# The last two batches' product of decayed scores and v: plain float32 in place of bfloat16 pieces

## The chip, the cores and the metric

The kernel runs on one core of a Trainium2 chip. A core has TensorE (PE, matmuls; its weight loads are listed apart as PEld), VectorE (DVE), ScalarE (ACT), GpSimd (POOL) and SyncE (SP, which here only issues DMAs). Each engine works through its own instructions in the order in which the program gives them and waits on semaphores for the others; the DMA queue of SP also issues in order. The metric is device microseconds of the whole program, lower is better.

## The reference, cut to what matters

A gated linear attention (mLSTM) over 4 batches, 8 heads, 768 steps, head size 40, followed by an MLP mixer over tokens and channels:

```python
for t in range(S):                       # per batch and head
    m_new = np.maximum(f[t] + m, i[t])
    f_s, i_s = np.exp(f[t] + m - m_new), np.exp(i[t] - m_new);  m = m_new
    C = f_s * C + i_s * outer(v[t], k[t])
    n = f_s * n + i_s * k[t]
    y[t] = sigmoid(o[t]) * (C @ q[t]) / np.maximum(abs(n @ q[t]), 1.0)
# x = y as (batch, 768, 320)
u = x + (relu(x.T @ w_tok1) @ w_tok2).T
out = u + relu(u @ w_ch1) @ w_ch2
```

All of it is float32. The changed step is a part of `C @ q[t]` (and `n @ q[t]`, which is a column of ones appended to v).

## The kernel before, in words

The recurrence is done in chunks of 128 steps, 6 chunks to a batch, 24 units `(b, c)` in all. For one unit: `st_s` multiplies k with q (scores, tile `ps_sc`, 8 heads) and lets DVE multiply them with the decays (tile `dd`, 128 x 8 x 128, made by ACT's exponentials in `prep_exp` from rows that a DMA spreads over the partitions, after POOL has masked them in `prep_mask`). `st_state` multiplies the state `C` with the decayed q (`q3t`, line 316, batches 0 and 1 only) and forms the chunk's own update `pu` from the decayed k (`kw`) and v (line 324), which DVE folds into the next state `Cn`. `st_pv` multiplies the decayed scores with v, per head a 128x128 stationary tile and 41 columns (40 of v and the ones), and adds the state's part; ACT copies the result to `ht`, POOL multiplies it with the output gate (`st_hs`), DVE divides and rounds it (`st_x`), POOL forms the rounding's rest `xl` for the MLP's matmuls.

Batches 0 and 1 do `st_pv` in plain float32 (line 364). Batches 2 and 3 (`three(u)` true) split both sides into bfloat16 pieces whose sum is the float32 number: DVE makes the rests of the scores (`prep_p2`, line 281; `prep_p3`, line 289) and the three pieces of v (`prep_v`, lines 297 to 300), and `st_pv3` runs four bfloat16 matmuls per head (line 345; two of 82 columns, two of 41) into two PSUM tiles, adds the state's part there (line 350), and ACT and DVE add the halves (lines 352, 353).

The MLP of a batch is one stream on PE: `a_part` and `phase_b` (token mixing), transposes, then 18 slots of `gemm1` (tile `ps_h`) and `gemm2` (tile `acc`). ACT and DVE make `gh` and `gl` out of `ps_h` in between, for the `gemm2` of the slot after. The attention of the next batch is a generator, `att`, with 5 steps per unit; a table, `STEPS`, says how many of them follow each `gemm1`. So batch 2's attention runs inside batch 1's MLP, batch 3's inside batch 2's, and the order on every engine is fixed by where the steps call their operations:

- step 1: `st_s` and its products; step 2: `st_state`; step 3: first half of the next unit's exponentials; step 4: `st_pv`, `st_hs`; step 5: second half of the exponentials, loads for the unit after the next.
- for batches 0 and 1 the next unit's `prep_q3` and `prep_kw` (ACT's exponential of `pq`; POOL's `decay`, `q3t`, `kw`) stand in step 3 and `st_x` in step 4. For batches 2 and 3 they stand in step 5, behind `prep_v` and `st_x`.

Buffers: `dd` has two buffers and a third under the name `p12`, which batches 2 and 3 use for the rest `r`; `pq`, `kw` and `ht` have one, `q3t` and the k and v tile `kvt` two, the PSUM tag `m` (for `po`, `pu`, `ps_b`, some transposes) two.

Of the kernel before, what the change touches and what calls it, by code (L numbers as in the profile page):

```python
# [7 lines left out]
F32 = mybir.dt.float32  # L8
F32R = mybir.dt.float32r
I32 = mybir.dt.int32  # L10
BF16 = mybir.dt.bfloat16
# [6 lines left out]
L = 128  # L18
# [15 lines left out]
def kernel(ctx: ExitStack, tc: tile.TileContext, gates, qk, q3, kv, og,  # L34
# [148 lines left out]
    def load_phi(u):  # L183
        b, c = u
        T.setdefault(u, {})
        third = b < 2 and c % 3 == 2
        dd = ap.tile([128, H, L], F32, tag="p12" if third else "dd", name="dd", bufs=1 if third else 2)
        if b:
            nc.sync.dma_start(out=dd, in_=phi_d[c, b * HP:b * HP + H].partition_broadcast(128))
        T[u]["dd"] = dd  # L190
# [79 lines left out]
    def three(u):  # L270
        return u[0] > 1

    def prep_p2(u):
        t = T[u]
        dd = t["dd"]
        r = ap.tile([128, H, L], F32, tag="p12", name="r", bufs=1)
        p3 = xpool[1].tile([128, H, L], BF16, tag="p3", name="p3", bufs=1)
        t["p"] = (top(dd), top(r), p3)
        for hf in range(2):
            h = slice(4 * hf, 4 * hf + 4)  # L280
            nc.vector.tensor_tensor(r[:, h], dd[:, h], top(dd)[:, h], ALU.subtract)
        t["r"] = r

    def prep_p3(u):
        t = T[u]
        r, p3 = t["r"], t["p"][2]
        for hf in range(2):
            h = slice(4 * hf, 4 * hf + 4)
            nc.vector.tensor_tensor(p3[:, h], r[:, h], top(r)[:, h], ALU.subtract)

    def prep_v(u):
        t = T[u]
        vx = t["kv"][:, DM:]
        w = xpool[1].tile([128, 3, H * E1], BF16, tag="v3", name="v3", bufs=1)
        r = ap.tile([128, H * E1], F32, tag="kw", name="vr", bufs=1)
        v = nc.vector
        v.tensor_copy(w[:, 0], vx)
        v.tensor_tensor(r, vx, w[:, 0], ALU.subtract)
        v.tensor_copy(w[:, 1], r)
        v.tensor_tensor(w[:, 2], r, w[:, 1], ALU.subtract)  # L300
        t["v"] = w

# [3 lines left out]
    def st_state(u):  # L306
# [4 lines left out]
        if c > 0 and not three(u):  # L311
            pool = (ps_acc, "acc") if b == 0 and c % 2 else (ps_m, "m")
            po = pool[0].tile([128, H, E1], F32, tag=pool[1], name="po")
            pof = po.rearrange("p h e -> p (h e)")
            for g, (h0, n) in enumerate(GR):
                nc.tensor.matmul(pof[:, h0 * E1:(h0 + n) * E1], t["q3"][0][0:n * D, g, :],  # L316
                                 Cst[b][0:n * D, g * G3:g * G3 + n * E1], start=g == 0, stop=False)
            t["po"] = po
# [17 lines left out]
    def st_pv3(u):  # L336
        b, c = u
        t = T[u]
        p, w = t["p"], t["v"].rearrange("p j (h e) -> p h j e", h=H)
        ht = ap.tile([128, H, E1], F32, tag="ht", name="ht", bufs=1)  # L340
        for h0, h1 in ((0, 6), (6, 8)):
            po = ps_m.tile([128, h1 - h0, 2, E1], F32, tag="m", name="po")
            for h in range(h0, h1):
                for i, j0, j1 in ((0, 0, 2), (1, 0, 2), (0, 2, 3), (2, 0, 1)):
                    nc.tensor.matmul(po[:, h - h0, 0:j1 - j0], p[i][:, ROW[h], :], w[:, h, j0:j1],  # L345
                                     start=h == h0 and i + j0 == 0,
                                     stop=c == 0 and h == h1 - 1 and i == 2)
            for g, (g0, n) in enumerate(GR):
                if c and h0 <= g0 < h1:
                    nc.tensor.matmul(po[:, g0 - h0:g0 - h0 + n, 0], t["q3"][0][0:n * D, g, :],  # L350
                                     t["C"][0:n * D, g * G3:g * G3 + n * E1], start=False, stop=g > 0)
            nc.scalar.activation(ht[:, h0:h1], po[:, :, 0], AF.Copy)
            nc.vector.tensor_tensor(ht[:, h0:h1], po[:, :, 1], ht[:, h0:h1], ALU.add)  # L353
        t["ht"] = ht

    def st_pv(u, copy=True):
# [3 lines left out]
        if "p" in t:  # L360
            return st_pv3(u)
# [71 lines left out]
    def att(b):  # L433
        for c in range(NC):
            u = (b, c)
            n1, n2 = after(u, 1), after(u, 2)
            th = three(u)
# [5 lines left out]
            if n2 and not three(u):  # L443
                load_phi(n2)
            if n1 and not three(u):
                prep_mask(n1)
            if n2:
                load_qk(n2, 0)
            if th:
                prep_p2(u)  # L450
            yield
            if th:
                prep_p3(u)
            st_state(u)
            if n1 and three(u):
                prep_mask(n1)
            yield
            if n1:
                prep_exp(n1, 0)
                if not three(n1):  # L460
                    prep_q3(n1)
                    prep_kw(n1)
# [5 lines left out]
            if not th:  # L468
                st_x(u)
            yield  # L470
            if n1 and three(n1):
                prep_v(n1)
            if th:
                st_x(u)
            if n1:
                if three(n1):
                    prep_q3(n1)
                    prep_kw(n1)
                prep_exp(n1, 1)
            if n2:  # L480
                load_kv(n2)
                load_q3(n2)
                if three(u):
                    load_phi(n2)
# [534 lines left out]
```

## Time and profile before

| | |
|---|---|
| median of 3 runs | 468.4 us (465.58, 468.4, 473.29) |
| profiled execution, its own time | 468.86 us |
| span of the profile | 467.0 us, granted PE clock 0.977 on average |
| PE busy | 445.9 us (95%) |
| DVE, ACT, POOL busy | 314.1, 178.2, 137.8 us |

The profile's first 130 us hold batch 0's attention and the decoding of the weights, and 130 to 180 us batch 1's attention inside batch 0's MLP. Batch 2's attention runs from 184 to 280 us, batch 3's from 280 to 382 us. After that comes batch 3's MLP alone. A matmul's own duration says little about its cost: matmuls are pipelined and several are under way at a time. What one costs is read from the starts, from its own to that of the matmul behind it. A float32 matmul leaves two records, so eight of them are listed as x16.

### The profile page before, as it was taken

The page shows a single profiled execution, that of the slowest core. Times are in us where ns is not written, and L with a number is a line of the kernel's source. Part 1 is how long each engine was busy: PE and PEld are TensorE (multiplying, and loading weights), DVE is VectorE, ACT ScalarE, POOL GpSimd, SP SyncE. Part 2 cuts the span into 40 slices and gives each one's busy share as a digit, 9 for nine tenths or more (in the row PEclk, how much of TensorE's full clock was granted, in tenths as well). Part 3 has the DMA queues.
Part 4 walks back from the last instruction along what each step waited for, and adds up shares of the span by engine and source line. Part 5 has one row for each costly group of instructions (what it writes and reads, how often), then busy time and mean ns, then how long its engine had stood idle before and what let it go on. Part 6 is the DMA issues. An engine that isn't in the chain of part 4 may idle for free.

```text
span 467.0 us, 9350 instructions
## 1 busy us (share of the span) xinstructions
PE 445.9 (95%) x3674; PEld 426.3 (91%) x3674; DVE 314.1 (67%) x688; ACT 178.2 (38%) x440; POOL 137.8 (29%) x164
## 2 busy tenths in 40 slices
PE   7699899998999999999999999999999999999997
PEld 3698799897999999999988999999988999999996
DVE  5857999999267666877797578877689565223322
ACT  4544643764544545433224324514323411212111
POOL 5636763444315434022234123023133120000000
PEclk9999758999999999999999999999999999999999
DMA  7746765664038882222533822240542100000000
GB/s 228 218 128 219 211 170 201 225 197 145 2 133 213 223 262 96 86 57 80 163 82 98 257 66 76 71 113 23 162 124 63 39 1 29 1 0 29 1 28 29
DMA packets 25032, 53.16 MB, mean 114 GB/s; under 512 B 2577, under 2 KB 13781, under 8 KB 24989
## 3 DMA queue, kind: packets, MB, share of 16 engines
q1 hardware_dynamic: 24941, 52.46, 37.3%
q8 instruction: 29, 0.48, 0.4%
q14 instruction: 14, 0.11, 0.1%
q10 hardware_dynamic: 48, 0.11, 0.1%
HBM read 48.51 MB, written 4.04 MB: 113 GB/s over the span
## 4 chain that ended last, share of the span: by engine, by line
PE 64%; DMA 11%; DVE 8%; issue 6%; POOL 5%; ACT 4%; SPq 1%; POOLq 0%; DVEq 0%; ACTq 0%
PE ps_h L582 18%; PE acc L582 18%; DMA dd<-phi_d 7%; PE ps_a L582 5%; PE po L364 5%; PE ps_b L582 4%; PE ps_sc L258 4%; PE pu L324 2%; DMA pq<-phi_d 2%; DVE wf L555 2%; PE po L316 2%; PE po L345 2%; POOL q3t L226 1%; POOL dd L230 1%; ACT dd L238 1%
## 5 line engine op out<-in xcount | busy, mean ns | idle before, releaser
L582 PE MATMUL ps_h<-uT,c1h 128*128 128x256 f32 x720 | 138.2, 280 | 0.1
L582 PEld LDWEIGHTS ps_h<-uT,c1h 128*128 128x128 f32 x720 | 115.1, 189 | 1.1 <-DVE uT L633 0.3
L582 PE MATMUL ps_h<-uT,c1l 128*128 128x256 f32 x432 | 110.2, 279 | 0.0
L650 DVE SCALAR_TENSOR_TENSOR gl<-ps_h,gh 128x512 fp32r<-128x512 f32 x72 | 49.5, 687 | 81.0 <-ACT gh L649 80.9
L649 ACT ACTIVATE gh<-ps_h 128x512 fp32r<-128x512 f32 x72 | 42.9, 596 | 159.4 <-PE ps_h L582 150.4
L582 PE MATMUL acc<-c2h,gh 128*128 128x320 f32 x288 | 90.3, 321 | 0.0
L582 PE MATMUL acc<-c2l,gh 128*128 128x320 f32 x288 | 86.6, 308 | 0.0
L582 PEld LDWEIGHTS ps_h<-uT,c1l 128*128 128x128 f32 x432 | 81.3, 188 | 0.0
L582 PE MATMUL acc<-c2h,gl 128*128 128x320 f32 x288 | 65.9, 310 | 3.0 <-DVE gl L650 3.0
L238 ACT ACTIVATE dd<-dd,bcol 128x128 f32<-128x128 f32 x144 | 45.9, 392 | 31.0 <-POOL dd L230 30.9
L582 PEld LDWEIGHTS acc<-c2h,gh 128*128 128x128 f32 x288 | 54.1, 188 | 1.3
L582 PEld LDWEIGHTS acc<-c2l,gh 128*128 128x128 f32 x288 | 54.2, 188 | 0.0
L582 PEld LDWEIGHTS acc<-c2h,gl 128*128 128x128 f32 x288 | 47.9, 188 | 4.5 <-DVE gl L650 4.5
L384 POOL TENSOR_TENSOR sig<-sig,ht 128x320 f32<-128x320 f32 x23 | 19.6, 851 | 78.6 <-DVE ht L353 64.2
L416 POOL TENSOR_TENSOR xl<-x,xh 128x320 fp32r<-128x320 f32 x23 | 21.1, 919 | 49.5 <-DVE xh L412 43.6
L230 POOL TENSOR_SCALAR_AFFINE_SELECT dd<-dd 128x1024 f32<-128x1024 f32 x18 | 20.7, 1150 | 49.1 <-DMA dd<-phi_d 42.9
L268 DVE TENSOR_TENSOR dd<-ps_sc,dd 128x512 f32<-128x512 f32 x48 | 31.1, 681 | 4.8 <-PE ps_sc L258 4.8
L258 PE MATMUL ps_sc<-raw 40*128 40x128 f32 x384 | 33.2, 310 | 0.7 <-DMA raw<-in_qk_dram 0.7
L258 PEld LDWEIGHTS ps_sc<-raw 40*128 40x128 f32 x384 | 28.1, 210 | 5.0 <-DMA raw<-in_qk_dram 1.7
L364 PE MATMUL po<-kvt,dd 128*128 128x41 f32 x192 | 29.7, 324 | 1.2 <-issue 1.2
L364 PEld LDWEIGHTS po<-kvt,dd 128*128 128x128 f32 x192 | 29.2, 239 | 1.6 <-issue 1.3
L324 PE MATMUL pu<-kvt,kw 128*120 128x123 f32 (+1 forms) x120 | 18.3, 295 | 4.9 <-POOL kw L248 4.8
(127 smaller groups left out, 775.7 us busy)
## 6 DMA issues: line engine op xcount, KB each, us to landing
dd<-phi_d SPq DMA_DIRECT2D x18, 512.0 KB
wst<-in_wc_dram SPq DMA_DIRECT2D x22, 384.0 KB
kvt<-in_kv_dram SPq DMA_DIRECT2D x24, 324.0 KB
raw<-in_qk_dram SPq DMA_DIRECT2D x48, 160.0 KB
sig<-in_og_dram SPq DMA_DIRECT2D x8, 480.0 KB
out_dram<-x SPq DMA_DIRECT2D x24, 160.0 KB
q3t<-in_q_dram SPq DMA_DIRECT2D x20, 180.0 KB
pq<-phi_d SPq DMA_DIRECT2D x18, 180.0 KB
```

Of the source, the lines that this page charges most:

```text
L230: nc.gpsimd.affine_select(dd, dd, pattern=[[0, H], [1, L]], compare_op=ALU.is_ge, fill=-1e30, base=0, channel_multiplier=-1)
L238: nc.scalar.activation(dd[:, h, :], src[hf][:, h % 4, :] if src else dd[:, h, :], AF.Exp, bias=bcol[:, c, HP * b + h:HP * b + h + 1])
L258: nc.tensor.matmul(t["s"][hf][:, h, :], r[:, 1, h, :], r[:, 0, h, :], start=True, stop=True)
L268: nc.vector.tensor_tensor(dd, t["s"][hf], dd, ALU.mult)
L316: nc.tensor.matmul(pof[:, h0 * E1:(h0 + n) * E1], t["q3"][0][0:n * D, g, :], Cst[b][0:n * D, g * G3:g * G3 + n * E1], start=g == 0, stop=F ...
L324: nc.tensor.matmul(pu[0:n * D, g, 0:n * E1], kwf[:, h0 * D:(h0 + n) * D], vx[:, h0 * E1:(h0 + n) * E1], start=True, stop=True)
L364: nc.tensor.matmul(po[:, h, :], t["dd"][:, ROW[h], :], vx[:, h * E1:(h + 1) * E1], start=c == 0 and h == 0, stop=h == H - 1)
L384: (nc.vector if u == (0, NC - 1) else nc.gpsimd).tensor_tensor(sg, sg, ht[:, :, 0:D], ALU.mult)
L416: (nc.vector if u == (0, 4) else nc.gpsimd).tensor_tensor(xl, x, f32(xh), ALU.subtract)
L582: nc.tensor.matmul(ps, a, m, start=(first and i == 0), stop=(last and i == n - 1))
L649: nc.scalar.activation(gh, ps, AF.Relu)
L650: nc.vector.scalar_tensor_tensor(gl, ps, 0.0, f32(gh), op0=ALU.max, op1=ALU.subtract)
```

## The change

`three`, `prep_p2`, `prep_p3`, `prep_v` and `st_pv3` are gone. All batches use `st_state` and `st_pv` as batches 0 and 1 did, and all units have the order of steps that batch 1 had: `prep_mask` and the load of `dd` in step 1, `prep_q3` and `prep_kw` in step 3, `st_x` in step 4. `dd` has three buffers of one tag throughout.

```diff
--- before.py
+++ after.py
@@ -183,8 +183,7 @@
     def load_phi(u):
         b, c = u
         T.setdefault(u, {})
-        third = b < 2 and c % 3 == 2
-        dd = ap.tile([128, H, L], F32, tag="p12" if third else "dd", name="dd", bufs=1 if third else 2)
+        dd = ap.tile([128, H, L], F32, tag="dd", name="dd", bufs=3)
         if b:
             nc.sync.dma_start(out=dd, in_=phi_d[c, b * HP:b * HP + H].partition_broadcast(128))
         T[u]["dd"] = dd
@@ -267,39 +266,6 @@
             dd = t["dd"][:, 4 * hf:4 * hf + 4, :]
             nc.vector.tensor_tensor(dd, t["s"][hf], dd, ALU.mult)
 
-    def three(u):
-        return u[0] > 1
-
-    def prep_p2(u):
-        t = T[u]
-        dd = t["dd"]
-        r = ap.tile([128, H, L], F32, tag="p12", name="r", bufs=1)
-        p3 = xpool[1].tile([128, H, L], BF16, tag="p3", name="p3", bufs=1)
-        t["p"] = (top(dd), top(r), p3)
-        for hf in range(2):
-            h = slice(4 * hf, 4 * hf + 4)
-            nc.vector.tensor_tensor(r[:, h], dd[:, h], top(dd)[:, h], ALU.subtract)
-        t["r"] = r
-
-    def prep_p3(u):
-        t = T[u]
-        r, p3 = t["r"], t["p"][2]
-        for hf in range(2):
-            h = slice(4 * hf, 4 * hf + 4)
-            nc.vector.tensor_tensor(p3[:, h], r[:, h], top(r)[:, h], ALU.subtract)
-
-    def prep_v(u):
-        t = T[u]
-        vx = t["kv"][:, DM:]
-        w = xpool[1].tile([128, 3, H * E1], BF16, tag="v3", name="v3", bufs=1)
-        r = ap.tile([128, H * E1], F32, tag="kw", name="vr", bufs=1)
-        v = nc.vector
-        v.tensor_copy(w[:, 0], vx)
-        v.tensor_tensor(r, vx, w[:, 0], ALU.subtract)
-        v.tensor_copy(w[:, 1], r)
-        v.tensor_tensor(w[:, 2], r, w[:, 1], ALU.subtract)
-        t["v"] = w
-
     Cst = {}
     GR = ((0, 3), (3, 3), (6, 2))
 
@@ -308,7 +274,7 @@
         t = T[u]
         vx = t["kv"][:, DM:]
         t["C"] = Cst.get(b)
-        if c > 0 and not three(u):
+        if c > 0:
             pool = (ps_acc, "acc") if b == 0 and c % 2 else (ps_m, "m")
             po = pool[0].tile([128, H, E1], F32, tag=pool[1], name="po")
             pof = po.rearrange("p h e -> p (h e)")
@@ -333,32 +299,10 @@
                                                    op0=ALU.mult, op1=ALU.add)
             Cst[b] = cn
 
-    def st_pv3(u):
-        b, c = u
-        t = T[u]
-        p, w = t["p"], t["v"].rearrange("p j (h e) -> p h j e", h=H)
-        ht = ap.tile([128, H, E1], F32, tag="ht", name="ht", bufs=1)
-        for h0, h1 in ((0, 6), (6, 8)):
-            po = ps_m.tile([128, h1 - h0, 2, E1], F32, tag="m", name="po")
-            for h in range(h0, h1):
-                for i, j0, j1 in ((0, 0, 2), (1, 0, 2), (0, 2, 3), (2, 0, 1)):
-                    nc.tensor.matmul(po[:, h - h0, 0:j1 - j0], p[i][:, ROW[h], :], w[:, h, j0:j1],
-                                     start=h == h0 and i + j0 == 0,
-                                     stop=c == 0 and h == h1 - 1 and i == 2)
-            for g, (g0, n) in enumerate(GR):
-                if c and h0 <= g0 < h1:
-                    nc.tensor.matmul(po[:, g0 - h0:g0 - h0 + n, 0], t["q3"][0][0:n * D, g, :],
-                                     t["C"][0:n * D, g * G3:g * G3 + n * E1], start=False, stop=g > 0)
-            nc.scalar.activation(ht[:, h0:h1], po[:, :, 0], AF.Copy)
-            nc.vector.tensor_tensor(ht[:, h0:h1], po[:, :, 1], ht[:, h0:h1], ALU.add)
-        t["ht"] = ht
-
     def st_pv(u, copy=True):
         b, c = u
         t = T[u]
         vx = t["kv"][:, DM:]
-        if "p" in t:
-            return st_pv3(u)
         po = t["po"] if c else ps_m.tile([128, H, E1], F32, tag="m", name="po")
         for h in range(H):
             nc.tensor.matmul(po[:, h, :], t["dd"][:, ROW[h], :], vx[:, h * E1:(h + 1) * E1],
@@ -434,54 +378,36 @@
         for c in range(NC):
             u = (b, c)
             n1, n2 = after(u, 1), after(u, 2)
-            th = three(u)
             if b + 1 < B and c in (3, 4):
                 load_sig(b + 1, c - 3)
             if b > 1 and c == 0:
                 sigmoid(b)
             st_s(u)
-            if n2 and not three(u):
+            if n2:
                 load_phi(n2)
-            if n1 and not three(u):
+            if n1:
                 prep_mask(n1)
             if n2:
                 load_qk(n2, 0)
-            if th:
-                prep_p2(u)
             yield
-            if th:
-                prep_p3(u)
             st_state(u)
-            if n1 and three(u):
-                prep_mask(n1)
             yield
             if n1:
                 prep_exp(n1, 0)
-                if not three(n1):
-                    prep_q3(n1)
-                    prep_kw(n1)
+                prep_q3(n1)
+                prep_kw(n1)
             if n2:
                 load_qk(n2, 1)
             yield
             st_pv(u)
             st_hs(u)
-            if not th:
-                st_x(u)
+            st_x(u)
             yield
-            if n1 and three(n1):
-                prep_v(n1)
-            if th:
-                st_x(u)
             if n1:
-                if three(n1):
-                    prep_q3(n1)
-                    prep_kw(n1)
                 prep_exp(n1, 1)
             if n2:
                 load_kv(n2)
                 load_q3(n2)
-                if three(u):
-                    load_phi(n2)
             yield
 
     def prep_first(u, n):
```

Two places where the order moves. The first is GpSimd, in batch 2, between the mask of one unit (`dd`) and the next; `sig` is `st_hs`, `xl` belongs to `st_x`, and `decay`, `q3t` and `kw` are made for the next unit. Before:

```order
L230 AFFINE_SELECT dd<-dd 128x1024
L384 TENSOR_TENSOR sig<-sig,ht 128x320
L416 TENSOR_TENSOR xl<-x,xh 128x320
L225 COPY decay<-pq 120x3
L226 TENSOR_TENSOR q3t<-q3t,pq 120x384
L248 TENSOR_TENSOR kw<-kvt,wcol 128x320
```

The change:

```order
L229 AFFINE_SELECT dd<-dd 128x1024
L224 COPY decay<-pq 120x3
L225 TENSOR_TENSOR q3t<-q3t,pq 120x384
L247 TENSOR_TENSOR kw<-kvt,wcol 128x320
L328 TENSOR_TENSOR sig<-sig,ht 128x320
L360 TENSOR_TENSOR xl<-x,xh 128x320
```

The next unit's `decay`, `q3t` and `kw` now come ahead of this unit's `sig` and `xl`, which need the result of `st_pv` and DVE's division.

The second place is TensorE in batch 2, unit (2, 1), steps 1 and 2. Before:

```order
L258 MATMUL ps_sc<-raw 128x128 x8
L324 MATMUL pu<-kvt,kw 120x123 x2
L324 MATMUL pu<-kvt,kw 80x82
L582 MATMUL acc_2458<-c2h,gh 128x320
L582 MATMUL acc_2458<-c2l,gh 128x320
```

The change:

```order
L257 MATMUL ps_sc<-raw 128x128 x8
L282 MATMUL po<-Cn,q3t 128x123 x2
L282 MATMUL po<-Cn,q3t 128x82
L290 MATMUL pu<-kvt,kw 120x123 x2
L290 MATMUL pu<-kvt,kw 80x82
L508 MATMUL acc_2412<-c2h,gh 128x320
```

The state's part (`po`) moves from among the bfloat16 matmuls of `st_pv3` to ahead of `pu`. At `st_pv` itself eight rows of float32 matmuls (128x41) stand where 32 bfloat16 ones were.

## Rows read from the trace of the kernel before

**Rows 1.** Windows: us, busy time (count) per engine, granted PE clock, DMA share, GB/s

```profile
130.00:180.00 50.00, 48.65 (x431) 46.34 (x430) 32.76 (x82) 22.83 (x66) 19.11 (x24) 1.00 0.71 205
180.00:284.00 104.00, 101.75 (x962) 98.52 (x961) 78.22 (x179) 39.49 (x98) 26.98 (x32) 1.00 0.37 112
284.00:384.00 100.00, 97.50 (x923) 95.23 (x922) 74.44 (x170) 32.91 (x86) 25.85 (x31) 1.00 0.25 72
```

**Rows 2.** Waits, 180 to 385 us: us in total, times, longest

```profile
PE pu L324 <- POOL kw L248: 4.8, 6, 1.1
...
PEld pu L324 <- POOL kw L248: 6.0, 6, 1.4
PEld ps_b L582 <- DVE rl L600: 0.4, 2, 0.2
```

**Rows 3.** Timeline of PE, unit (2, 2): start, duration, instruction, count

```profile
228.56 0.21 PE L345 MATMUL po<-v,dd 128*128 128x82 bf16 x1
...
229.33 0.69 PE L350 MATMUL po<-Cn,q3t 120*128 120x123 f32 x4
...
230.11 0.43 PE L350 MATMUL po<-Cn,q3t 80*128 80x82 f32 x2
230.34 0.39 PE L582 MATMUL acc<-c2h,gh 128*128 128x320 f32 x1
```

**Rows 4.** Timeline of PE, unit (2, 0), 32 bfloat16 matmuls between these

```profile
197.68 0.21 PE L345 MATMUL po<-v,dd 128*128 128x82 bf16 x1
...
198.71 0.39 PE L582 MATMUL acc<-c2h,gh 128*128 128x320 f32 x1
```

**Rows 5.** Timeline of PE, batch 1, units (1, 1) and (1, 3)

```profile
143.20 1.87 PE L364 MATMUL po<-kvt,dd 128*128 128x41 f32 x16
144.90 0.39 PE L582 MATMUL acc<-c2h,gh 128*128 128x320 f32 x1
...
157.80 0.79 PE L316 MATMUL po<-Cn,q3t 120*128 120x123 f32 x6
158.43 0.77 PE L324 MATMUL pu<-kvt,kw 128*120 128x123 f32 x6
159.03 1.92 PE L364 MATMUL po<-kvt,dd 128*128 128x41 f32 x16
```

**Rows 6.** Timeline of PE, one of the six waits for kw

```profile
358.39 0.83 PE L324 MATMUL pu<-kvt,kw 128*120 128x123 f32 x6 [0.90 <-POOL kw L248]
```

**Rows 7.** Timeline of POOL, the same stretch

```profile
355.23 0.88 POOL L416 TENSOR_TENSOR xl<-x,xh 128x320 fp32r<-128x320 f32 x1 [2.80 <-DVE xh L412]
...
356.19 1.02 POOL L226 TENSOR_TENSOR q3t<-q3t,pq 120x384 f32<-120x384 f32 x1
357.17 1.17 POOL L248 TENSOR_TENSOR kw<-kvt,wcol 128x320 f32<-128x320 f32 x1
```

**Rows 8.** Groups of DVE by shape: count, busy us, mean ns, idle before

```profile
L281 DVE TENSOR_TENSOR r<-dd 128x512 f32<-128x512 f32 x24 | 21.4, 929 | 0.0
...
L298 DVE TENSOR_TENSOR vr<-kvt,v 128x328 f32<-128x328 f32 x12 | 10.5, 874 | 1.5 <-DVE v L297 0.5
```

**Rows 9.** Timelines of SP, ACT and PE, unit (1, 5)

```profile
163.17 0.74 SPq L214 DMA_DIRECT2D pq<-phi_d  x1
...
171.77 0.53 ACT L222 ACTIVATE pq<-pq 120x384 f32<-120x384 f32 x1 [2.96 <-DMA pq<-phi_d]
...
175.69 2.08 PE L364 MATMUL po<-kvt,dd 128*128 128x41 f32 x16 [1.21 <-issue]
177.60 0.39 PE L582 MATMUL acc<-c2h,gh 128*128 128x320 f32 x1
```

**Rows 10.** Groups of PE by shape, whole span

```profile
L364 PE MATMUL po<-kvt,dd 128*128 128x41 f32 x192 | 29.7, 324 | 1.2 <-issue 1.2
...
L345 PE MATMUL po<-v,dd 128*128 128x82 bf16 x96 | 13.9, 200 | 0.0
...
L345 PE MATMUL po<-v,p 128*128 128x41 bf16 x96 | 13.3, 181 | 0.0
```

## The prediction

> **What bounds the kernel now.** I read the windows first, then the waits of TensorE in the stretch that the change touches, then TensorE's timeline there, and the other engines last. The windows [rows 1] are to show whether TensorE has anything to give away where batches 2 and 3 do their attention, 180 to 384 us. It has not: it is busy 101.75 of 104 and 97.50 of 100 us, at the full granted clock (1.00), while DVE is busy 75%, ACT 35% and POOL 26% of that time. Idle are 204 - 199.25 = 4.75 us, and the waits [rows 2] say what for: six waits for POOL's `kw`, 4.8 us together on the matmuls and 6.0 us on the weight loads ahead of them, nothing else on the matmuls' side. DVE, from which the change takes the most, does not appear there, but for 0.4 us before `ps_b`. So this stretch is issued by TensorE almost without a break, and the change has to be priced in what TensorE issues, plus those waits.
>
> **TensorE: what the product costs.** Durations of single matmuls mislead here; they overlap. The four bfloat16 groups of the 12 units add up to about 54 us of busy time (two like each of the two shown, 13.9 and 13.3), the float32 group of the other 12 units to 29.7 [rows 10]; read as costs, these would say that float32 is the cheaper by half. Starts tell otherwise.
>
> - Unit with c = 0 (2 of the 12): 32 bfloat16 matmuls go from 197.68 to 198.71, 1.03 us [rows 4]. Eight float32 ones, 16 records, go from 143.20 to 144.90, 1.70 us [rows 5]. That is +0.67 us, twice: +1.3.
> - Unit with c > 0 (10 of the 12): bfloat16 matmuls and the state's part together take 228.56 to 230.34, 1.78 us [rows 3]. After the change the state's part runs in one piece ahead of `pu`, as it does from 157.80 to 158.43, 0.63 us [rows 5], and the unit pays 0.63 + 1.70 = 2.33 us. That is +0.55 us, ten times: +5.5.
>
> Together TensorE issues 6.8 us more. The price of the float32 group is bounded by other places of the same line: 1.70 us is the lowest, 177.60 - 175.69 = 1.91 us behind a stall is the highest [rows 9], which would be 12 x 0.21 = 2.5 us more. I take 1.70, since in batches 2 and 3 the group follows a `gemm1` as it does at 143.20, and with no stall ahead of it.
>
> **TensorE: which waits go.** `kw` is late before because POOL takes it last of a row of five: `xl` first waits 2.80 us for DVE's rounding, and `q3t` and `kw` follow it, so that `kw` ends at 358.34 and `pu` starts at 358.39, 0.90 us late [rows 6, 7]. DVE's rounding in turn stands behind the splitting of v. After the change `q3t` and `kw` come in step 3, ahead of `st_pv` and of everything that needs its result, and `pu` uses `kw` in step 2 of the next unit. That is at least one slot of the MLP later, mostly two, so all six waits should go: -4.8 us by the one row, -6.0 by the other, and I take the middle, -5.4. The 0.4 us before `ps_b` [rows 2] are the MLP's `rl` behind the rests of scores on DVE; those are gone too: -0.4.
>
> **DVE, ACT, POOL: nothing on the path.** DVE loses its largest groups there, 21.4 and 10.5 us among them [rows 8], and the smaller ones of the split; ACT loses one of two copies per unit; POOL has as many operations as before in another order. No wait of TensorE's names DVE's split, but for those counted, so I cost this at nothing: what covered it is TensorE's own stream.
>
> **What is moved and waits anew.** `prep_q3` goes from step 5 to step 3. Its first operation, ACT's exponential of `pq`, waits for a DMA, and behind it on ACT are now the copy `ht` of this unit, the second half of the next unit's exponentials and the next `gh`; behind POOL's `q3t` are `kw` and `st_hs`, and DVE's `x` waits for that. With `pq` in time this costs nothing: the next `gl` is wanted by `gemm2` a whole slot later. `st_x` in step 4 makes DVE wait for ACT and POOL right behind `st_pv`, in front of the next `gl`; the same slot covers it. The load of `dd` in step 1 finds a free buffer of three, where two had to wait for `st_pv`; SP passes it ahead of the scores' operands instead of behind `pq`, and POOL's mask, one unit later, has that unit's time. The PSUM tile `po` is now held from step 2 to step 4; between these steps the table puts no other user of that tag but `pu`, which takes the second buffer. For batches 0 and 1 the third buffer is only renamed.
>
> **The sum.** 6.8 - 5.4 - 0.4 = +1.0 us on the profiled execution's 468.86 us (span 467.0): **469.9 us**, 1.5 us over the median of the runs shown. By the bounds above: 469.3 to 473.0.
>
> **A rule against the row.** The group of eight float32 matmuls has 192 records for 96 matmuls [rows 10], so two of 106 ns each per head [rows 5]. The Trainium skill (FP8 and Floating Point Precision, section TensorE Precision Notes) says that true float32 takes four passes through the array. With a weight load for each pass at the row's 106 ns the unit would pay 3.4 us, and the sum would be 12 x 1.7 = 20 us higher, 490 us. The trace shows two records, not four, and I go by it; 1% for more than two.
>
> **Rivals.**
>
> 1. **The wait for POOL stays.** POOL's three operations for the next unit now wait for ACT and `pq`, and `pu` and the state's matmuls wait for both `q3t` and `kw`. If step 3's POOL work still ends behind step 2 of the next unit, the 5.4 us stay: 475.3 us. Against it: POOL is busy a quarter of the time [rows 1], and has a slot more. 13%.
> 2. **`pq` comes late (slower).** In unit (1, 5) this order shows its weak side: `pq` issued at 163.17, ACT waits 2.96 us for it and begins at 171.77, 8.6 us after the issue, and the exponentials and the product behind it leave TensorE idle for 1.21 us ahead of `st_pv` [rows 9]. If each of the ten units with c > 0 does so, 12.1 us: 482.0 us. It decides where landing takes longer than the way from step 5 to step 3 of the next unit. For it: the order is the same. Against it: batch 1's units follow each other after (159.03 - 143.20) / 2 = 7.9 us [rows 5], batch 2's after (228.56 - 197.68) / 2 = 15.4 us [rows 3, 4], and the DMA share is 0.37 and 0.25 there, 0.71 in batch 1 [rows 1]. 6%.
> 3. **DVE's relief gives more than the waits show.** The weight loads idle 204 - 193.75 = 10.25 us; without the 6.4 us named, 3.8 us are left in short gaps. If they all came from a crowded DVE, 466.1 us. Against it: no row names it. 11%.
> 4. **Columns set the price (faster).** If a matmul cost what it streams, 4 x 41 = 164 columns a head against 246, the group would take 1.03 x 164 / 246 = 0.69 us, 12 x 1.01 us less than I count: 457.8 us. The two records at 106 ns each speak flatly against it [rows 5]. 2%.
>
> **Range and chances.** My case has 67%, at 469.9 us. 464.5 to 476 us takes in its bounds, rivals 1 and 3, and what the runs of one kernel differ by (the three shown lie 2.8 us under and 4.9 us over their median); rivals 2 and 4 stay out. Two per cent, about what a measurement can tell from no change, are 9.4 us: under 459.0 us only rival 4 and an unforeseen gain, 3%; over 477.8 us rival 2 and the four passes, 7%; within, 90%.
>
> **What would show it.** In the profile of the changed kernel: line 308 from its first start to the next line's, 1.70 us in batches 2 and 3 as in batch 1; line 282 ahead of `pu` at 0.63 us; no wait of `pu` for `kw` after 180 us; TensorE busy all but some 1 us there, and the stretch up to the last attention about 1 us longer; DVE's busy time lower by more than the 31.9 us of [rows 8], with no effect on the span. The prediction is wrong if TensorE idles ahead of `po` or `st_pv`, if ACT waits for `pq` by several us in batches 2 and 3, or if the float32 groups there start at another pace.

## The result, and the profile after

The changed kernel takes 471.04 us, the median of 20 runs (469.2 to 477.06), the kernel before 469.52 us in 20 runs beside it. The ratio is 1.0059, with a 95% interval of 1.0031 to 1.0087: 2.8 us more by the ratio, the same by the bound of 2%. (It is taken without the runs that lie over 1.5% above the fastest of their kernel, and is not the ratio of the two medians, 1.0032.) The forecast was 469.9 us in a range of 464.5 to 476 us, on a net cost of 1.0 us.

The profiled execution took 469.2 us (span 467.4), against 468.86. That difference of 0.3 us is not the change's alone: ahead of 180 us the runs differ by some microseconds, whichever kernel it is. I therefore compare the stretch that the change touches, from the first score matmul of unit (2, 0) to the first `ps_a` of batch 3's MLP: 183.94 to 383.97 us before, 181.66 to 384.39 us after, so 200.03 and 202.73 us, **2.70 us more**. What follows it to the end takes 83.07 and 82.99 us.

The page's first part, for the kernel after:

```profile
PE 447.1 (96%) x3482; PEld 429.7 (92%) x3482; DVE 264.0 (56%) x568; ACT 177.0 (38%) x428; POOL 135.5 (29%) x164
```

DVE has lost 314.1 - 264.0 = 50.1 us of work, and the kernel is no faster. The windows of [rows 1], after (the second and third cover nearly all of the stretch):

```profile
130.00:180.00 50.00, 49.57 (x438) 47.65 (x439) 33.15 (x79) 25.09 (x68) 21.25 (x27) 1.00 0.73 214
180.00:284.00 104.00, 103.03 (x858) 101.11 (x857) 52.05 (x116) 37.55 (x90) 25.85 (x33) 1.00 0.34 107
284.00:384.00 100.00, 99.03 (x816) 97.58 (x816) 48.47 (x109) 31.37 (x79) 21.61 (x28) 1.00 0.23 72
```

TensorE idles 204 - 202.06 = 1.94 us there, where it idled 4.75 us. It waits less and takes longer: it has more to issue. All that it waits for between 180 and 385 us, to be held against [rows 2]:

```profile
PEld pu L290 <- issue: 2.2, 2, 1.1
PE pu L290 <- DVE uT L560: 1.9, 2, 1.0
...
PEld ps_sc L257 <- issue: 0.6, 3, 0.2
```

No wait for `kw` is left, and none for `rl`. In their place stands something new: `pu`, twice, behind DVE's `uT`, which is a tile of the MLP. TensorE's timeline shows the product: the group of unit (2, 0), which answers to [rows 4], and steps 2 and 4 of unit (2, 2), which answer to [rows 3]:

```profile
194.94 1.87 PE L308 MATMUL po<-kvt,dd 128*128 128x41 f32 x16
196.64 0.39 PE L508 MATMUL acc<-c2h,gh 128*128 128x320 f32 x1
...
221.97 0.79 PE L282 MATMUL po<-Cn,q3t 120*128 120x123 f32 x6
...
226.90 1.88 PE L308 MATMUL po<-kvt,dd 128*128 128x41 f32 x16
228.60 0.39 PE L508 MATMUL acc<-c2h,gh 128*128 128x320 f32 x1
```

From start to start the float32 group takes 1.70 us in both, 16 records of 106 ns. Summed over the stretch, each instruction from its own start to the next one's, TensorE's time by tile is:

| tile | before, us | after, us | difference |
|---|---|---|---|
| `po` (product and state's part) | 19.90 | 29.44 | +9.54 |
| `ps_h` | 71.45 | 67.72 | -3.73 |
| `ps_t` | 5.92 | 3.76 | -2.16 |
| `pu` | 6.04 | 5.60 | -0.44 |
| `ps_b` | 11.38 | 10.91 | -0.47 |
| `acc`, `ps_sc`, `ps_a` | 85.33 | 85.29 | -0.04 |

The waits for `kw` lay behind whatever stood ahead of `pu`, `ps_h` or `ps_t`, so that their end shows there: -6.33 us with `pu` itself. 5.7 us of that are the six gaps ahead of `pu`, 0.75 to 1.40 us from start to start before and 0.11 or 0.12 us where nothing is waited for. Of the +9.54 us, 2.27 are the new wait and 7.27 the product with the state's part. In unit 3 of batch 2 the new wait stands between lines 282 and 290; TensorE first, then DVE:

```profile
237.75 0.27 PE L557 MATMUL ps_t<-id_t,xd 128*128 128x128 f32 x1
237.86 0.80 PE L282 MATMUL po<-Cn,q3t 120*128 120x123 f32 x6
239.62 0.80 PE L290 MATMUL pu<-kvt,kw 128*120 128x123 f32 x6 [0.97 <-DVE uT L560]
240.22 0.39 PE L508 MATMUL acc<-c2h,gh 128*128 128x320 f32 x1
```

```profile
238.04 0.69 DVE L576 SCALAR_TENSOR_TENSOR gl<-ps_h,gh 128x512 fp32r<-128x512 f32 x1 [3.05 <-ACT gh L575]
238.64 0.41 DVE L559 TENSOR_TENSOR uT<-ps_t,uT 128x256 fp32r<-128x256 f32 x1
239.07 0.29 DVE L560 TENSOR_TENSOR uT<-ps_t,uT 64x128 fp32r<-64x128 f32 x1
239.40 0.42 DVE L559 TENSOR_TENSOR uT<-ps_t,uT 128x256 fp32r<-128x256 f32 x1
```

At slot 9, which falls into unit 3 of either batch, the MLP transposes its block 4 into a buffer of PSUM tag `m`, just ahead of step 2. `po` takes the tag's other buffer, and `pu` has to wait for the first until DVE has read it: line 290 starts 1.76 us behind line 282 and not 0.63. Before the change `po` was opened only in step 4, and `pu` found the second buffer free: where its `kw` is early (e1_early_kw, below), it starts 0.11 us behind the transposes in the same unit.

### The profile page after: what moved, and what is told of

Its sections match the earlier page's. It is cut to its first block, busy times and chain, and to the rows that moved or that the text cites. A ratio compares the mean times of both kernels' runs of the same rounds, so it can differ in the third digit from the quotient of the medians.

```text
span 467.4 us, 8794 instructions
## 1 busy us (share of the span) xinstructions
PE 447.1 (96%) x3482; PEld 429.7 (92%) x3482; DVE 264.0 (56%) x568; ACT 177.0 (38%) x428; POOL 135.5 (29%) x164
## 4 chain that ended last, share of the span: by engine, by line
PE 83%; DMA 5%; DVE 5%; ACT 3%; issue 2%; POOL 1%; SPq 1%; ACTq 0%; DVEq 0%; POOLq 0%
PE ps_h L508 25%; PE acc L508 25%; PE po L308 10%; PE ps_sc L257 6%; PE ps_b L508 4%; PE ps_a L508 4%; PE po L282 3%; PE pu L290 3%; DVE wf L481 2%; DMA wst<-in_wt_dram 2%; DMA kvt<-in_kv_dram 2%; DMA raw<-in_qk_dram 1%; ACT wf L465 1%; DVE wf L485 1%; DMA wst<-in_wc_dram 1%
## 5 line engine op out<-in xcount | busy, mean ns | idle before, releaser
L308 PE MATMUL po<-kvt,dd 128*128 128x41 f32 x384 | 50.6, 296 | 0.3 <-ACT gh L575 0.3
L308 PEld LDWEIGHTS po<-kvt,dd 128*128 128x128 f32 x384 | 50.1, 210 | 0.7 <-ACT gh L575 0.4
L224 POOL COPY decay<-pq 120x3 f32<-120x3 f32 x16 | 4.4, 274 | 117.6 <-ACT pq L221 117.6
L360 POOL TENSOR_TENSOR xl<-x,xh 128x320 fp32r<-128x320 f32 x23 | 21.3, 925 | 24.7 <-DVE xh L356 21.5
L225 POOL TENSOR_TENSOR q3t<-q3t,pq 120x384 f32<-120x384 f32 x15 | 15.5, 1037 | 21.2 <-ACT pq L221 21.2
```

The lines of the kernel that those rows point to most:

```text
L225: (nc.vector if u[0] == 1 else nc.gpsimd).tensor_tensor(q3t, q3t, pq, ALU.mult)
L308: nc.tensor.matmul(po[:, h, :], t["dd"][:, ROW[h], :], vx[:, h * E1:(h + 1) * E1], start=c == 0 and h == 0, stop=h == H - 1)
L360: (nc.vector if u == (0, 4) else nc.gpsimd).tensor_tensor(xl, x, f32(xh), ALU.subtract)
```

## The experiments

All ratios are to the kernel before on the same chip. "Stretch" is the one defined above (before 200.03, after 202.73 us), each from one profile.

| run | ratio | 95% interval | stretch, us |
|---|---|---|---|
| e1_early_kw | 0.9922 | 0.9888 to 0.9956 | 195.37 |
| e2_old_order | 1.0071 | 1.0036 to 1.0107 | 203.12 |
| e3_other_bank | 1.0033 | 1.0002 to 1.0065 | 200.41 |
| e4_split_kept | 1.0179 | 1.0134 to 1.0225 | 205.67 |
| e5_f32_twice | 1.0615 | 1.0544 to 1.0685 | 227.27 |
| e6_bf16_twice | 1.0165 | 1.0114 to 1.0217 | 206.06 |
| e7_two_dd | 1.0072 | 1.0037 to 1.0108 | 202.68 |
| e8_early_kw_calm | 0.9899 | 0.9862 to 0.9936 | 195.37 |
| e9_other_bank_calm | 0.9994 | 0.9959 to 1.0029 | 200.47 |
| e10_early_kw_shift | 0.9935 | 0.9905 to 0.9965 | 196.17 |
| e11_shift32 | 1.0078 | 1.0045 to 1.0111 | 203.97 |
| e12_split_kept_clean | 1.0105 | 1.0053 to 1.0158 | 203.02 |

### The two halves apart: the order alone, the product alone

e1_early_kw is the kernel before with its bfloat16 pieces, and only `prep_q3` and `prep_kw` moved to step 3 (`vr` gets a buffer of its own, since it used that of `kw`):

```diff
                 prep_exp(n1, 0)
-                if not three(n1):
-                    prep_q3(n1)
-                    prep_kw(n1)
+                prep_q3(n1)
+                prep_kw(n1)
...
-                if three(n1):
-                    prep_q3(n1)
-                    prep_kw(n1)
                 prep_exp(n1, 1)
```

> Edit alone of the order: the kernel before, bfloat16 pieces and all, with prep_q3 and prep_kw of batches 2 and 3 in step 3 instead of step 5 (the rest of v, vr, gets a buffer of its own, since kw now lives across prep_v). My theory, that the changed kernel pays 6.8 us for the float32 product and gets most of it back from POOL's late kw: the six waits of pu go, 5.4 us less than the kernel before, ratio 0.988, and no wait comes in their place. Rival, that the waits go only when DVE loses the split: POOL's q3t and kw stay as late as they were or pass the wait on, ratio 1.000.

The stretch is 4.66 us shorter than before, and the run takes 0.8% less, between the theory's 0.988 and the rival's 1.000. TensorE's waits in it:

```profile
PEld L345 <- DVE p L289: 0.5, 2, 0.3
PEld ps_b L578 <- DVE rl L596: 0.4, 2, 0.2
...
PE po L345 <- DVE p L289: 0.3, 2, 0.2
```

The waits for `kw` are gone and 0.3 us for the pieces have come. So the order alone removes them, and nothing of float32 is needed for it. It does not show in full: by tiles, `po` takes 0.65 us more than before, and `gemm1` some 1.1 us more for another reason ("where the operands lie", below).

e2_old_order is the other half: the float32 product with before's order of steps.

```diff
+                if n1 and th1:
+                    prep_q3(n1)
+                    prep_kw(n1)
                 prep_exp(n1, 1)
```

> Edit alone of the product: the changed kernel's float32 product and three buffers, with the old order of steps for batches 2 and 3 (mask in step 2, prep_q3, prep_kw and st_x in step 5, load of dd in step 5). Theory A, that the order takes the waits away: kw is late as before, so +6.8 us for the product and some 2 us for the state's matmuls that wait for a PSUM buffer in unit 3, ratio 1.015 to 1.02. Theory B, that the split's leaving DVE takes them away too, since the 2 us of the split of v stood ahead of the division that POOL waits for: the waits of 0.6 to 1.4 us are all shorter than those 2 us, so they go, ratio 1.003 to 1.008 like the changed kernel.

The run is 0.7% slower than before. Its waits:

```profile
PEld pu L290 <- issue: 2.2, 2, 1.1
PE pu L290 <- DVE uT L572: 1.9, 2, 1.0
PEld po L282 <- POOL q3t L225: 0.6, 2, 0.3
```

No wait for `kw` either: with the split off DVE, the rounding that POOL's `xl` waits for comes early enough by itself. POOL's row of [rows 7] in the same unit, (3, 3):

```profile
356.89 0.88 POOL L360 TENSOR_TENSOR xl<-x,xh 128x320 fp32r<-128x320 f32 x1 [1.28 <-DVE xh L356]
```

It waits 1.28 us there and not 2.80, and in all ten units `kw` ends 3.7 us or more ahead of its `pu`. The prediction put the end of the waits down to the new order. Either half does it, and together they save it once.

### The new wait

```diff
-                9: [(phase_t, 4), (phase_t, 5, ss)]}
+                9: [(phase_t, 4, ss), (phase_t, 5, ss)]}
```

e3_other_bank is the kernel after with block 4's transposes in the PSUM pool of the scores.

> The changed kernel with the transposes of block 4 (slot 9) in the scores' PSUM tag instead of the tag m. In the changed kernel pu of unit 3 waits 1.1 us in each of batches 2 and 3 behind po. My theory: ps_t of block 4 holds the second buffer of m until DVE has read it, and po has taken the first. Then these two waits go, 2.2 us less than the changed kernel, ratio to the kernel before 1.001. Rival, that pu waits for DVE or POOL for another reason (kw, or DVE's queue): the two waits stay, ratio 1.006.

The stretch is 2.32 us shorter than after, and line 290 follows line 282 after 0.63 us in the same unit:

```profile
244.21 0.80 PE L282 MATMUL po<-Cn,q3t 120*128 120x123 f32 x6
244.84 0.77 PE L290 MATMUL pu<-kvt,kw 128*120 128x123 f32 x6
```

That is shown, then: the second buffer of tag `m` was taken. The intervals of e3_other_bank and after overlap; the verdict rests on the trace.

e7_two_dd takes back the third buffer of `dd`, the other part of the change:

```diff
-        dd = ap.tile([128, H, L], F32, tag="dd", name="dd", bufs=3)
+        third = b < 2 and c % 3 == 2
+        dd = ap.tile([128, H, L], F32, tag="p12" if third else "dd", name="dd", bufs=1 if third else 2)
```

> The changed kernel with two buffers for the decays in batches 2 and 3, as before (batches 0 and 1 keep three), all else as changed: the third buffer undone alone. The load of dd for the unit after the next then waits on SP's queue until st_pv of this unit, three steps later, and what is behind it on SP waits too. My theory, that a unit of 15 us leaves time for that: as the changed kernel, ratio 1.004 to 1.008, TensorE without new waits. Rival, that the held queue delays the scores' operands or the mask, and with it ACT's exponentials: TensorE waits for raw or for the product, ratio 1.012 or more.

The stretch is that of after to 0.05 us, with the same two waits for `uT` and the same three short waits of the scores' loads, 0.6 us together. The third buffer is worth nothing here.

### What each product costs, by doubling it

e5_f32_twice issues the float32 group of batches 2 and 3 twice (kernel after), e6_bf16_twice the bfloat16 groups (kernel before):

```diff
+        n = 2 if b > 1 else 1
+        for i in range(n):
+            for h in range(H):
+                nc.tensor.matmul(po[:, h, :], t["dd"][:, ROW[h], :], vx[:, h * E1:(h + 1) * E1],
...
+            for k in range(2):
+                for h in range(h0, h1):
```

> The changed kernel with the eight float32 matmuls of the product issued twice in batches 2 and 3 (the output then has that product twice). My theory, that TensorE's issue is the bound there: 12 x 1.70 = 20.4 us more than the changed kernel, ratio to the kernel before 1.049. Rival, that the group hides behind other work or other waits (part of its 1.70 us is the pipeline's latency and not paid again): less than 15 us more, ratio under 1.038.

> The kernel before with the 32 bfloat16 matmuls of the product issued twice in batches 2 and 3 (the output then has that product twice). By the starts in the trace 12 x 1.03 = 12.4 us more, ratio 1.026; POOL's kw, which the longer unit gives more time, may take back one or two us of it, ratio 1.022. By the busy times of the groups (54 us for the bfloat16 matmuls against 30 us for float32 ones) it would be more than for float32, ratio over 1.05.

The doubled groups of unit (2, 0), for bfloat16, and of a unit of batch 3, for float32:

```profile
199.38 0.21 PE L346 MATMUL po<-v,dd 128*128 128x82 bf16 x1
...
201.41 0.40 PE L583 MATMUL acc<-c2h,gh 128*128 128x320 f32 x1
```

```profile
309.45 3.66 PE L310 MATMUL po<-kvt,dd 128*128 128x41 f32 x32
312.94 0.39 PE L510 MATMUL acc<-c2h,gh 128*128 128x320 f32 x1
```

2.03 us against 3.49. A second group costs 1.00 us in bfloat16 and 1.79 us in float32, so that 12 units differ by 12 x 0.79 = 9.5 us if nothing hides a part. (The prediction's 6.8 us are for one group each, 12 x 0.67 = 8.0 us, less 1.2 us that it gains on the state's part.) The order is that of the prediction's pricing by starts, and the opposite of what the busy times of [rows 10] say (54 against 29.7 us). Both runs missed their expected ratios. e6_bf16_twice lost its waits for `kw` to the longer groups, so that its stretch grew by 6.0 us and not by the 12.1 us that `po` takes more. e5_f32_twice is slower than the groups alone make it: 21.7 of its 24.5 us are theirs, and twice, of 12 such groups, the granted clock fell near the end of one: once 0.4 us behind the group, once 0.5 us before it was over. The first time, in windows with the columns of [rows 1]:

```profile
309.00:313.00 4.00, 4.00 (x38) 4.00 (x36) 1.31 (x3) 0.38 (x1) 0.00 (x0) 1.00 0.00 0
313.40:316.60 3.20, 3.20 (x15) 3.20 (x14) 1.87 (x5) 1.40 (x5) 1.59 (x2) 0.50 0.55 178
317.00:321.00 4.00, 4.00 (x34) 4.00 (x33) 1.32 (x3) 0.98 (x2) 0.73 (x1) 1.00 0.61 216
```

TensorE never paused. Behind the 32 records its clock stands at 0.50, so 1.2 of 2.4 GHz, and the trace has 15 matmuls in 3.2 us where the next window has 34 in 4. Most of the other 3 us are `acc` (2.5 us more than after), which follows the groups.

### DVE's relief

e4_split_kept is the kernel after with the split still made by DVE, and used by nobody; e12_split_kept_clean is the same on top of e3_other_bank, with `vr` 32 bytes longer. The calls, with the old functions put back:

```diff
+            if b > 1:
+                prep_p2(u)
             yield
+            if b > 1:
+                prep_p3(u)
...
+            if n1 and n1[0] > 1:
+                prep_v(n1)
```

> The changed kernel with DVE's splitting of scores and v left in for batches 2 and 3, at its old places, its results unused (some 61 us of DVE's time back). My theory, that DVE's relief is worth nothing once kw comes in step 3: as the changed kernel, ratio 1.004 to 1.008, TensorE without new waits. Rival, that the relief gave part of what was won back: 3.8 us slower than the changed kernel or more, ratio 1.014 or more, and TensorE waits for DVE (gl, the product with the decays, or a PSUM tile).

> The changed kernel with the transposes of block 4 in the scores' PSUM tag (ratio 1.003 by itself) and DVE's splitting of scores and v left in, unused, its buffer vr 32 bytes longer so that uT begins where it does in the changed kernel. It asks again what DVE's relief is worth, without the two things that came with it before (the wait for the PSUM buffer, longer when DVE is busier, and the place of uT). My theory: only the 0.4 us ahead of ps_b come back, ratio 1.003 to 1.006. Rival, that a busy DVE holds TensorE up: 3 us more, ratio 1.010 or more.

The first was a poor experiment. Its stretch is 2.94 us longer than after's: the wait for `uT` has grown by 1.25 us (its row says 3.2 us where after's says 1.9), `ps_b` costs 0.50 us more, and `gemm1` (`ps_h`) 1.09 us, which has nothing to do with DVE: e11_shift32 (below), which has no split, spends the same on it (68.82 us in the stretch against 68.81). The ratio says more than this, 5.6 us over after; 0.8 us of them lie behind the stretch, and the rest I could not place. The second separates them better: 2.61 us over e3_other_bank, of which 2.01 are `ps_h`, 0.48 `ps_b` behind `rl` and 0.19 `ps_t`. Its ratio is that of the rival, but its `gemm1` is not after's, as the longer `vr` was to make it: it has the slowest of the three paces, and behind the stretch too, where no split runs (34.8 us of `ps_h` against 33.5). I therefore leave `ps_h` out, by this argument and not by a run. Then DVE's relief is worth some 0.7 us beside the waits for `kw`, near the 0.4 us of [rows 2], and rival 3 is far off.

### A side effect: where the operands lie

The 16 records of one group of `gemm1` take another time in some of these kernels, with the same instructions. By the start of `uT` in its partition, as the programs were built, there are three paces. e10_early_kw_shift makes `vr` 32 bytes longer in e8_early_kw_calm (below), e11_shift32 puts 32 unused bytes ahead of the MLP's tiles in the kernel after:

```diff
-        r = ap.tile([128, H * E1], F32, tag="vr", name="vr", bufs=1)
+        r = ap.tile([128, H * E1 + 8], F32, tag="vr", name="vr", bufs=1)[:, 0:H * E1]
...
+    pad = lp.tile([128, 8], F32, tag="pad", name="pad", bufs=1)
+    nc.gpsimd.memset(pad, 0.0)
```

> The kernel before with early kw, two buffers for pq and the output gate's loads moved (ratio 0.990), with its new buffer vr 32 bytes a partition longer. In the three kernels with vr the 16 records of gemm1 take 1.89 us instead of 1.84 even after the last attention, where no other edit reaches; there uT and gh begin at a multiple of 64 bytes in their partition, in the others 32 bytes past one. Theory, that the place of the operands sets that pace: 1.84 us again, 0.8 us less after the last attention and 1.1 us less in batches 2 and 3, ratio 0.985 to 0.988. Rival, that DVE's work or chance sets it: 1.89 us, ratio 0.990.

> The changed kernel with an unused tile of 32 bytes a partition ahead of the MLP's tiles (rh, rl, uT, gh, gl and xd lie 32 bytes further, nothing else is touched). By the theory of the place: gemm1's 16 records 1.89 us instead of 1.84, 1.1 us more in batches 2 and 3 and 0.8 us after, and as much in batch 1's share of the MLP, ratio 1.010. By the rival nothing changes, ratio 1.006.

One group of `gemm1` behind the stretch, start to the start of the `gemm2` behind it, in the kernel after (1.83 us) and in e11_shift32 (1.89 us):

```profile
425.43 0.28 PE L508 MATMUL ps_h<-uT,c1h 128*128 128x256 f32 x1
...
427.26 0.31 PE L508 MATMUL acc<-c2h,gh 128*128 128x320 f32 x1
```

```profile
424.76 0.28 PE L508 MATMUL ps_h<-uT,c1h 128*128 128x256 f32 x1
...
426.65 0.31 PE L508 MATMUL acc<-c2h,gh 128*128 128x320 f32 x1
```

Over the stretch and what follows, `ps_h` takes 1.10 and 0.80 us more in e11_shift32, all other tiles together 0.13 and 0.04: by the traces the shift costs 2.1 us, 1.9 of them in `ps_h`. The ratio cannot decide it, since its interval holds both expected values. My rule for it, that a start at a multiple of 64 bytes is slow, fell with e10_early_kw_shift, which was to be faster and has a slower `gemm1` still (34.8 us behind the stretch; after 33.5, e11_shift32 34.3). That the place counts is shown; by what rule stays open. The programs as built give a lead: `uT` begins 96 bytes past a multiple of 128 in its partition in the eight kernels with the fastest pace, at a multiple of 128 in the four with the middle one (e1_early_kw, e4_split_kept, e8_early_kw_calm, e11_shift32) and 32 bytes past one in the two with the slowest (e10_early_kw_shift, e12_split_kept_clean). That sorts them all, but it was read off afterwards, and the MLP's other tiles moved along. Before and after have the fast one both, so it has no part in the result.

### Both versions at their best

e8_early_kw_calm and e9_other_bank_calm add to e1_early_kw and e3_other_bank what helps unit (1, 5) of [rows 9]: a second buffer for `pq`, and the loads of `sig` in other units.

```diff
-            pq = ap.tile([120, 3, L], F32, tag="pq", name="pq", bufs=1)
+            pq = ap.tile([120, 3, L], F32, tag="pq", name="pq", bufs=2)
...
-            if b + 1 < B and c in (3, 4):
-                load_sig(b + 1, c - 3)
+            if b + 1 < B and c in (1, 5):
+                load_sig(b + 1, c // 5)
```

> The kernel before with prep_q3 and prep_kw of batches 2 and 3 in step 3 (as in the run of the order alone, ratio 0.992), and with two buffers for pq and the loads of the output gate moved from units 3 and 4 of a batch to units 1 and 5, so that 480 KB less are under way when the decays pq of unit (1, 5) are loaded. Theory: the stall of 1.2 to 1.8 us ahead of st_pv of unit (1, 5), and the fall of the granted clock to half that follows it in some profiles, come from pq's DMA that lands 8.6 us after its issue. Then the stall shrinks to under 0.5 us, the clock holds after 130 us, ratio 0.985 to 0.989 and a narrower spread of the runs. Rival, that pq lands late for its own transfer's sake: the stall stays, ratio 0.992.

> The changed kernel with the transposes of block 4 in the scores' PSUM tag (ratio 1.003 by itself), two buffers for pq and the output gate's loads in units 1 and 5. By the theory that the late pq of unit (1, 5) costs 1.2 to 1.8 us and, in some runs, some us of halved clock: ratio 0.996 to 1.000, no wait over 0.5 us of st_pv at (1, 5). By the rival: ratio 1.003. Against the kernel with bfloat16 pieces and early kw and the same loads it should be slower by 5 us, the product's 6.8 us less what DVE's splitting costs there.

e8_early_kw_calm takes 464.49 us, less than both kernels (1.0%; not 2%), a little short of the expected 0.985 to 0.989. ACT and TensorE at (1, 5), to be held against [rows 9]:

```profile
170.15 0.52 ACT L222 ACTIVATE pq<-pq 120x384 f32<-120x384 f32 x1 [0.86 <-DMA pq<-phi_d]
```

```profile
175.19 1.92 PE L364 MATMUL po<-kvt,dd 128*128 128x41 f32 x16
```

ACT's wait has shrunk from 2.96 to 0.86 us and TensorE's is gone. It has in part moved: two units earlier, at (1, 3), TensorE now waits 0.96 us for DVE's `dd` ahead of the product. What the two edits give by themselves is not shown, for the intervals with and without them overlap (e8_early_kw_calm and e1_early_kw, e9_other_bank_calm and e3_other_bank). The float32 version with the same edits, 468.1 us, is no better than the kernel before. The intervals of e8_early_kw_calm and e9_other_bank_calm do not overlap: without the wait for the buffer and with the same loads, the pieces are faster by 0.0095 of the time, some 4.5 us, with 5.1 us between the stretches, and that although their `gemm1` has the middle pace (1.8 us more in the stretch and behind it).

## Why the prediction was right, and where it was not

The time lay in the range and the likeliest case was the right one, since its two large terms held and were nearly of one size. The range alone proves little: 464.5 to 476 us would have held a change of nothing as well, and the forecast of +1.0 us lies under the interval that was measured (1.5 to 4.1 us). So it is the terms that have to be held against the runs, one by one:

- **TensorE bounds the stretch, and the change is priced in what it issues.** Right: 50.1 us less on DVE gave nothing beyond the waits, and 7.27 us more of issue cost as much.
- **The product, +6.8 us.** 7.27 measured. The group takes the 1.70 us taken from [rows 5] (1.70 or 1.71 in 11 of the 12 units, 1.80 in one), not the upper bound of 1.91. The state's part was sized a little low: 0.63 us in six of its ten units, counting unit 3 without its wait, but 0.73 in unit 1 and 0.69 in unit 5 of either batch.
- **The waits, -5.4 and -0.4 us.** -6.33 and -0.47 measured. The gaps alone, 5.7 us, lie between the two bounds for `kw`; the rest is in the matmuls beside them. The reason was half right: the new order suffices (e1_early_kw), but so does the split's leaving DVE (e2_old_order).
- **`po`, held from step 2 to step 4, costs nothing.** This is the step that failed. "Between these steps the table puts no other user of that tag but `pu`, which takes the second buffer" counts users between the steps, and not the one ahead of them that still holds the second buffer. It cost 2.27 us (e3_other_bank: 2.32). With it the sum is 7.27 + 2.27 - 6.33 - 0.47 = +2.7 us, the measured difference of the stretches, where I had +1.0. The other misses, +0.4, -0.9 and -0.1 us, took 0.6 us of that back, which is luck.
- **DVE's relief at nothing.** Nearly: 0.7 us (e12_split_kept_clean), of which 0.4 were counted with `rl`. (DVE does not lose its largest group there, as the prediction has it: `gl`, 24.7 us between 180 and 385 us, stays.)
- **The third buffer at nothing.** Right (e7_two_dd).
- **Rivals 1 and 2.** Neither came. POOL makes `kw` for the next unit 6.6 us before its `pu` starts at 358.44, where it ended 0.05 us before it [rows 6, 7]; ACT's waits after 184 us name `ps_h`, `po`, `ps_a` and `ps_t`, never `pq`. POOL in batch 3, and the `pu` that uses it:

```profile
350.09 1.01 POOL L225 TENSOR_TENSOR q3t<-q3t,pq 120x384 f32<-120x384 f32 x1
351.06 0.73 POOL L247 TENSOR_TENSOR kw<-kvt,wcol 128x320 f32<-128x320 f32 x1
```

```profile
358.44 0.77 PE L290 MATMUL pu<-kvt,kw 128*120 128x123 f32 x6
```

- **Columns, and four passes.** Both fall with one row of the page, 24 units of 8 matmuls in 384 records: two apiece, at 106 ns from start to start.

```profile
L308 PE MATMUL po<-kvt,dd 128*128 128x41 f32 x384 | 50.6, 296 | 0.3 <-ACT gh L575 0.3
```

A bfloat16 record with 41 or 82 columns follows the last one after 1.03 / 32 = 0.032 us [rows 4], a float32 one with 41 after 0.106 us, and those of the state's part, with 123 or 82, after 0.63 / 6 = 0.105 us [rows 5]. So at these sizes neither columns nor four passes set the price; it goes with the type of the operands. Whether it is the type of the weights or that of the columns no run shows, since both change together. The loads of 128 x 128 weights point to it, with a median of 192 ns in float32 and 97 in bfloat16 (minimum, median and longest):

```profile
L364 PEld LDWEIGHTS po<-kvt,dd x192: 186/192/338, 22.8 to 177.5; 128*128 128x128 f32 x192
L345 PEld LDWEIGHTS <-dd x192: 96/97/109, 197.7 to 381.8; 128*128 128x128 bf16 x192
```

The Trainium skill (TensorE: Matmul & The Clock Gate, section Weight-path perf modes) says that the fast weight load is on for 128 weights of any type but float32; the trace agrees as far as it goes, with bfloat16 records at 3.3 times the pace, and does not show the mode itself.

## What to carry to other kernels

Price a change of matmuls by the time from a group's own start to the next group's, and never by the busy times of pipelined records: here these named the dearer product the cheaper by half. Where a change adds issue on the engine that bounds and takes waits from it, run its two halves apart: the gain here could be had from the order of POOL's work alone, without the float32 product, for 0.8% less time (e1_early_kw). And when a tile of a rotating PSUM tag is opened earlier, go back over the table to the last taker of each buffer, not only forward to the next.

## What the runs showed that I had not expected

- **Behind a short stall of TensorE its clock can fall.** In e3_other_bank's profile ACT waits 3.14 us for `pq` at unit (1, 5), and TensorE idles 1.78 us ahead of the product. Then its granted clock falls to half, 1.2 GHz, though it is busy throughout (windows, columns as in [rows 1]):

```profile
171.00:177.80 6.80, 5.02 (x48) 4.55 (x47) 4.24 (x9) 2.50 (x7) 2.62 (x3) 1.00 0.65 209
178.00:184.60 6.60, 6.60 (x27) 6.60 (x27) 1.87 (x5) 6.03 (x12) 3.35 (x4) 0.50 0.50 149
185.00:190.00 5.00, 5.00 (x43) 4.69 (x43) 0.80 (x2) 0.00 (x0) 0.00 (x0) 1.00 0.26 81
```

  27 matmul records stand in 6.6 us at half the clock. It fell at this place in five other profiles as well, behind stalls of 1.8 us (e2_old_order, e4_split_kept, e11_shift32), 1.2 us (e6_bf16_twice) and 0.7 us (e7_two_dd), and stayed at 1.00 behind 1.25 us in e5_f32_twice, 1.21 us in before [rows 9], 0.86 us in e1_early_kw and 0.29 us in after; so the length of the stall alone does not decide. Where there was no such stall (e8_early_kw_calm, e9_other_bank_calm, e10_early_kw_shift, e12_split_kept_clean), it stayed at 1.00 there. In e10_early_kw_shift it fell earlier, at 160.1 us, behind a stall of 0.65 us in unit (1, 3), so that the edits meant to hold the clock do not always do so. Whether these falls make the spread of a kernel's runs was not shown: e9_other_bank_calm, whose profile has none between 71 us and its last microsecond, still took 466.08 to 473.09 us.
- **The clock also fell without a stall**, at the end of two of the twelve groups of some 3.5 us of float32 records with 41 columns (e5_f32_twice, above). In the stretch of the kernel after, with single groups of 1.70 us, it stayed at 1.00.
- **The place of an operand within its partition changes a matmul's pace**: mostly 1.84, 1.89 or 1.92 us for the same 16 records of `gemm1`, by shifts of multiples of 32 bytes. In a kernel with 54 such groups in the stretch and behind it, one shift of 32 bytes moved the time by 2.1 us (e11_shift32), which is most of what the change did.
